# Casts of keys and queries and a first addition of values moved from VectorE to GpSimd, in two of four batches

## The chip, the cores and the metric

The kernel runs on one core of a Trainium2 chip. The time is the device time of one execution in microseconds, as the median of several runs. A core has TensorE (PE in the profile), VectorE (DVE), ScalarE (ACT), GpSimd (POOL) and SyncE (SP); SP issues most of the DMAs here. Each engine works through its own queue in order and waits on semaphores for the others.

## The reference, cut to what matters

Clustered attention, then a gated feed-forward network on its result. A query sees only the keys whose nearest centroid is the same as its own.

```python
# q, k, v: (4 batches, 8 heads, 768 tokens, 64), centroids: (8, 16, 64)
q_assign = np.argmax(np.einsum('bhsd,hcd->bhsc', q_n, c_n), axis=-1)
k_assign = np.argmax(np.einsum('bhsd,hcd->bhsc', k_n, c_n), axis=-1)
mask = q_assign[:, :, :, None] == k_assign[:, :, None, :]
scores = np.where(mask, scale * np.matmul(q, k.transpose(0, 1, 3, 2)), -1e9)
attn = np.exp(scores - np.max(scores, axis=-1, keepdims=True))
attn = attn / (np.sum(attn, axis=-1, keepdims=True) + 1e-09)
x = np.matmul(attn, v)            # then to (3072 tokens, 512)
gate = 1.0 / (1.0 + np.exp(-(x @ w_gate)))     # w_gate, w_val: (512, 1536)
out = (gate * (x @ w_val)) @ w_out             # w_out: (1536, 512)
```

## The kernel before

**Work and stages.** The four batches run one after the other, and in each four pairs of heads. A pair is 24 steps of attention, 12 a head in most cases; a step takes one block of 128 keys against 384 queries. PE computes scores (`sc`, L1066), ACT the exponentials (`es`, L1071), and PE the product with the values (`av`, L1089). After the last step of a head VectorE adds the precomputed sum of values to `av` (`t`, L372) and takes reciprocals (`rec`, L374), and GpSimd multiplies (the normalisation, `xp`, L377). SP transposes `xp` by DMA into `xTb` (L1120), from which the feed-forward network of the batch reads. Its matmuls (gate `g`, L532; value `v`, L548; output `o`, L865 and L994) fill the room between the attention steps of the next batch. The last batch ends with a closing part of its own from about 271 us on.

**Preparation of a pair.** Each of the pairs of the batches 2 to 4 (numbered b = 1 to 3 in the program), but for the first pair of b = 1, is prepared some 60 steps ahead by `pair_prep`. For each head e and side (keys, queries) `sp` splits the f32 input into a high half in f16 and the rest, side by side in one tile `hl`: a cast (L1631, 128 x 6 x 64 elements) and a subtraction (L1632, GpSimd) that reads the cast's result. `turn` transposes the whole `hl` by one DMA from SP into `T` (L412). PE multiplies `T` with the centroids (`lg`, L436 or L423), VectorE reduces and picks the nearest centroid (`lgs` L451, `mx` L462, `oh` L464 and L471), and SP transposes that by DMA (`ohT`, L1649) and copies its rows into `T` (L492), where they serve as additional rows of the score matmul. Scores of the pair then read `T`.

**Values.** `v_cast` casts a pair's values to f16 (`va`, L324, GpSimd). `v_sum` adds the six blocks of values of a pair in parts: `one` adds the first three blocks to the last three (L332), `two` adds the three results (L338, L339), and `rest` sums over partitions with a matmul (L343) and scales the result (L348). All of `one` and `two` run on VectorE.

**What sets the order.** The program is written out step by step. The table `SCHED` says by how many steps each piece of the preparation comes ahead of the pair's first use: an entry such as `b2p1sp10` for one pair, else `b2sp10` for b = 2 and 3, else a default. `sp` names a split, with head and side as its digits. Pieces due at a step are issued between that step's scores and the next. Each engine's queue holds its instructions in the order in which they are issued so. Inputs come in three buffers of each kind, `hl` has four. PSUM banks for scores, `lg`, `g` and `v` come from a ring of four, so that a matmul waits for whoever reads the bank used four allocations before.

Of the kernel before, what the change touches and what calls it, by code (L numbers as in the profile page):

```python
# [11 lines left out]
ALU = mybir.AluOpType  # L12
# [83 lines left out]
    "fwv": [354, 356, 357, 359, 364, 366, 370, 371], "b3p2pk1": -28.5, "END": 0,  # L96
}


# [1 line left out]
def kernel(  # L101
# [12 lines left out]
    PE, ACT, DVE, POOL, SP = nc.tensor, nc.scalar, nc.vector, nc.gpsimd, nc.sync  # L114
# [205 lines left out]
    def v_cast(b, p, cast=None, e=None):  # L320
        va = VA[b, p] = vas[(b * NP + p) % len(vas)]
        h = slice(0, 2) if e is None else slice(e, e + 1)
        done.update(("v", b, p, i) for i in range(2)[h])
        (cast or POOL.tensor_copy)(va[:, h, :, 0:64], RAW["v", b, p][:, h])  # L324

    def v_sum(b, p, eng=None):
        r, st = RAW["v", b, p], {}
        eng = eng or DVE

        def one():  # L330
            st["a"] = vsp.tile([128, 2, 3, 64], FP, tag="va3", name="va3")
            eng.tensor_tensor(st["a"], r[:, :, 0:3], r[:, :, 3:6], ALU.add)  # L332

        def two():
            a = st["a"]
            s = st["s"] = vss[(b * NP + p) % len(vss)]
            t = vsp.tile([128, 2, 64], FP, tag="va1", name="va1")
            eng.tensor_tensor(t, a[:, :, 0], a[:, :, 1], ALU.add)  # L338
            eng.tensor_tensor(s[:, :, 0:64], t, a[:, :, 2], ALU.add)  # L339

        def rest():
            t = (turns if SCHED.get(f"vso{b}{p}", SCHED.get(f"vso{p}", 0)) else bank)(130, FP, name="vs_ps")
            PE.matmul(  # L343
                out=t, lhsT=ones, rhs=st["s"].rearrange("p h d -> p (h d)"), start=True, stop=True
            )
            sv = svp.tile([128, 2, 65], FP, tag="sv", name="sv")
            SV[b, p] = sv
            DVE.tensor_scalar(sv.rearrange("p h d -> p (h d)"), t, TINY, None, ALU.mult)  # L348

        return one, two, rest  # L350
# [59 lines left out]
    def turn(key, hl, pl):  # L410
        T[key] = pl.tile([128, hl.shape[1], 128], HP, tag="T", name="T")
        SP.dma_start_transpose(out=T[key], in_=hl.rearrange("p c x -> p (c x)"))  # L412

    def logits2(groups, sep=False):

        lg = (turns if SCHED.get("lgop", 1) else bank)(512, FP, name="lg2")
        lx = sep and SCHED.get("lx", 0)
        seq = [(i, s) for i in range(len(groups)) for s in range(2)]
        if lx:
            seq = [(i, s) for s in range(2) for i in range(len(groups))]  # L420
        for i, s in seq:
            t, c, h = groups[i]
            PE.matmul(  # L423
                out=lg[:, bass.ts(i, NCL)], lhsT=t[:, c, :], rhs=cm[:, h, s, :],
                start=(i == 0 and s == 0), stop=(s == 1), skip_group_check=True,
            )
        return lg[:, 0 : len(groups) * NCL].rearrange("p (c n) -> p c n", n=NCL)

    def logits(t, h, n, copy=None):
        return logits1([(t, c, h) for c in range(n)], copy)  # L430
# [25 lines left out]
    def pick(lg, parts):  # L456

        if isinstance(lg, tuple):
            lg = join(*lg)
        n = lg.shape[1]  # L460
        mx = smp.tile([128, 18], FP, name="mx")
        DVE.tensor_reduce(mx[:, 0:n], lg, AX.X, ALU.max)  # L462
        for a, z, nh, key, o in parts:
            DVE.tensor_tensor(  # L464
                o,
                lg[:, a:z].rearrange("p (h c) n -> p h c n", h=nh),
                bcast(mx[:, a:z].rearrange("p (h c) -> p h c", h=nh), NCL),
                ALU.is_equal if key else ALU.is_lt,
            )
            if not key:  # L470
                DVE.tensor_scalar(o, o, MASK, None, ALU.mult)  # L471
# [4 lines left out]
    def new_oh():  # L476
        oh_n[0] += 1
        return ohs[oh_n[0] % 3]

    def oh_view(oh, slot, nh, step, nc_):  # L480

        v_ = oh.rearrange("p c (s x) -> p s c x", x=32)
        return v_[:, slot : slot + (nh - 1) * step + 1 : step, 0:nc_, 0:NCL]
# [7 lines left out]
    def hop(src, slot, t, c0, n):  # L491
        SP.dma_start(  # L492
            out=t[64:80, c0 : c0 + n, :], in_=src[32 * slot : 32 * slot + 16, 0:n, :]
        )
# [630 lines left out]
    def at(i, f):  # L1125
        bg.setdefault(max(i, step_no[0] - 0.5), []).append(f)
# [11 lines left out]
    def need(*names):  # L1138
        for n in names:
            assert n in done, n  # L1140
# [361 lines left out]
    a = P[0, 0, 0]  # L1502
# [121 lines left out]
    def pair_prep(b, p, use):  # L1624
        st = {}

        def sp(e, side):
            if side == 0:
                st["hl", e] = hlp.tile([128, 12, 128], HP, tag="hl", name="hl")
            hl, r = st["hl", e][:, 6 * side : 6 * side + 6], RAW["kq"[side], b, p][:, e]  # L1630
            DVE.tensor_copy(hl[:, :, 0:64], r)  # L1631
            POOL.tensor_tensor(hl[:, :, 64:128], r, hl[:, :, 0:64], ALU.subtract)  # L1632

        def lgt(e):
            t, h = T[b, 2 * p + e], 2 * p + e
            if SCHED.get(f"b{b}p{p}l2{e}", 0):
                st["lg", e] = logits2([(t, c, h) for c in range(12)])
            else:
                st["lg", e] = logits(t, h, 12, SCHED.get(f"b{b}p{p}le{e}", 0) and DVE.tensor_copy)

        def pk(e):
            if e == 0:
                st["oh"] = new_oh()
            pick(st["lg", e], [(0, 6, 1, True, oh_view(st["oh"], 2 * e, 1, 1, 6)),
                               (6, 12, 1, False, oh_view(st["oh"], 2 * e + 1, 1, 1, 6))])

        def ot():
            st["ot"] = ohp.tile([128, NCH, 128], HP, tag="ohT", name="ohT")
            SP.dma_start_transpose(out=st["ot"], in_=st["oh"].rearrange("p c x -> p (c x)"))  # L1649

        def hops(e):
            if SCHED.get("hop2", 0):
                SP.dma_start(
                    out=T[b, 2 * p + e][64:80].rearrange("x (s c) t -> s x c t", s=2),
                    in_=st["ot"].rearrange("(y x) c t -> y x c t", x=32)[2 * e : 2 * e + 2, 0:16],
                )
                return
            for s in range(2):
                hop(st["ot"], 2 * e + s, T[b, 2 * p + e], 6 * s, 6)

        def go(name, off, f):
            o = SCHED.get(f"b{b}p{p}{name}", SCHED.get(f"b2{name}", off) if b > 1 else off)

            def g():
                if name[:2] == "tn":
                    need((b, p, f"sp{name[2]}0"), (b, p, f"sp{name[2]}1"))
                if name == "ot":
                    need((b, p, "pk0"), (b, p, "pk1"))
                f()
                done.add((b, p, name))  # L1670

            at(use + o, g)

        for e in range(0 if (b, p) in PEP else 2):
            o = -58 + 10 * e
            go(f"sp{e}0", o, lambda e=e: sp(e, 0))
            go(f"sp{e}1", o + 4, lambda e=e: sp(e, 1))
            go(f"tn{e}", o + 9, lambda e=e: turn((b, 2 * p + e), st["hl", e], tp))
            go(f"lg{e}", o + 20, lambda e=e: lgt(e))
            go(f"pk{e}", o + 21, lambda e=e: pk(e))  # L1680
        if (b, p) not in PEP:
            go("ot", -26, ot)
            go("hp0", -16, lambda: hops(0))
            go("hp1", -15, lambda: hops(1))
        go("vc", -20, lambda: v_cast(b, p))
        go("vs", -10, lambda: (st.update(f=v_sum(b, p)), st["f"][0]()))
        go("vu", -8, lambda: st["f"][1]())
        go("vt", -6, lambda: st["f"][2]())
# [13 lines left out]
    for b in range(B):  # L1702
# [17 lines left out]
        for p, e, c in heads(b):  # L1720
            for s in head_steps(b, p, e, c):
# [4 lines left out]
                r = step_no[0] - BASE[b]  # L1726
# [44 lines left out]
```

## Time and profile before

| | |
|---|---|
| median of 3 runs | 319.14 us (319.08 to 319.54) |
| the profiled execution | 319.12 us, its span 317.3 us |
| PE | 310.0 us busy, 98% of the span |
| weight loads (PEld, beside PE) | 218.8 us, 69% |
| VectorE (DVE) | 238.6 us, 75% |
| ScalarE (ACT) | 244.9 us, 77% |
| GpSimd (POOL) | 120.9 us, 38% |
| granted TensorE clock | 1.00 throughout |

In a row of a timeline the first number is the start in us from the span's beginning, the second the duration; "x3" merges three equal instructions, and "[4.99 <-PE sc L1066]" gives the idle time of that engine before it and what ended that. In a row of groups stand the busy time in us and the mean length of one in ns, then the idle time before them. For DMAs a row of SP (SPq) is the time it takes to issue; when the data have landed is told apart.

### The profile page before, as it was taken

To read this page: it belongs to the slowest core of one execution; us is meant where nothing else is said; L and a number is where in the kernel's file an instruction comes from. 1 tells how busy PE (TensorE), PEld (TensorE's weight loads), DVE (VectorE), ACT (ScalarE), POOL (GpSimd) and SP (SyncE) were. 2 spreads that over 40 slices of the span, in tenths; PEclk is the share of its full clock that TensorE was granted. 3 is DMA by queue.
4 is the path that set the end of the run, shared out by engine and by line. 5 is a ranking of instruction groups with operands and counts; after the bars stand their busy time and mean duration, and the time that the engine had idled before them with its cause. 6 is when DMAs were issued, how large, how long until landed. Compare 5 with 4: busy or idle time off the path is not lost.

```text
span 317.3 us, 9228 instructions
## 1 busy us (share of the span) xinstructions
PE 310.0 (98%) x3492; PEld 218.8 (69%) x3492; DVE 238.6 (75%) x623; ACT 244.9 (77%) x555; POOL 120.9 (38%) x157
## 2 busy tenths in 40 slices
PE   7899999999999999999999999999999999999995
PEld 4688766766666666666777678766677678656685
DVE  5899756778688777686788688776888776678983
ACT  6688998797899887877776876777877887588621
POOL 5888454244434275423234333424212111026600
PEclk9999999999999999999999999999999999999999
DMA  7999998639848988976676455882506130300014
GB/s 196 379 259 169 271 164 143 176 83 264 242 100 163 204 221 136 199 217 161 106 193 153 151 118 134 248 153 53 112 2 76 55 27 14 145 1 3 0 35 165
DMA packets 77996, 45.16 MB, mean 142 GB/s; under 512 B 56896, under 2 KB 75520, under 8 KB 77952
## 3 DMA queue, kind: packets, MB, share of 16 engines
q1 hardware_dynamic: 73840, 39.66, 51.3%
q0 software_dynamic: 3680, 4.72, 9.1%
q8 instruction: 27, 0.44, 0.6%
q10 hardware_dynamic: 432, 0.20, 0.2%
q14 instruction: 17, 0.14, 0.1%
HBM read 28.34 MB, written 6.29 MB: 109 GB/s over the span
## 4 chain that ended last, share of the span: by engine, by line
PE 93%; DMA 2%; DVE 1%; POOL 1%; SPq 1%; issue 0%; ACT 0%; DVEq 0%
PE sc L1066 19%; PE g L532 15%; PE v L548 15%; PE av L1089 11%; PE o L994 9%; PE o L865 5%; PE lg L436 2%; PE o L699 2%; PE o_end L802 2%; PE av L699 2%; DMA kraw<-in_k_dram 2%; PE v L628 2%; PE y L699 2%; PE o L802 1%; PE av L802 1%; PE z L699 1%
## 5 line engine op out<-in xcount | busy, mean ns | idle before, releaser
L1071 ACT ACTIVATE es<-sc 128x384 f16<-128x384 f32 x384 | 174.1, 492 | 38.5 <-PE sc L1066 29.8
L1066 PE MATMUL sc<-T 128*128 128x384 f16 x384 | 117.3, 325 | 0.7 <-DVE T L1396 0.4
L1089 PEld LDWEIGHTS <-es 128*128 128x128 f16 x1152 | 81.3, 98 | 35.1 <-ACT es L1071 0.2
L1089 PE MATMUL av<-va,es 128*128 128x65 f16 x1152 | 97.6, 194 | 0.0
L553 DVE SCALAR_TENSOR_TENSOR hT<-th,v 128x384 f16<-128x384 f32 x72 | 39.8, 553 | 33.8 <-PE av L1089 29.6
L377 POOL TENSOR_TENSOR xp<-t,rec 128x384 f16<-128x384 f32 (+1 forms) x30 | 21.8, 726 | 97.3 <-DVE rec L374 49.2
L548 PE MATMUL v<-xTb,wv 128*128 128x384 f16 x288 | 58.5, 326 | 0.1
L532 PE MATMUL g<-xTb,wg 128*128 128x384 f16 x288 | 58.5, 326 | 0.0
L538 ACT ACTIVATE th<-g 128x384 f32<-128x384 f32 x72 | 35.4, 492 | 8.3 <-PE g L532 6.3
L1066 PEld LDWEIGHTS <-T 128*128 128x128 f16 x384 | 37.0, 96 | 1.2 <-DVE T L1396 0.7
L548 PEld LDWEIGHTS <-wv 128*128 128x128 f16 x288 | 28.0, 97 | 13.9 <-issue 0.3
L532 PEld LDWEIGHTS <-wg 128*128 128x128 f16 x288 | 27.9, 97 | 13.9
L1632 POOL TENSOR_TENSOR hl<-kraw,hl 128x384 f16<-128x384 f32 x22 | 20.2, 920 | 40.6 <-DVE hl L1631 25.9
L1632 POOL TENSOR_TENSOR hl<-qraw,hl 128x384 f16<-128x384 f32 x22 | 21.1, 961 | 11.1 <-DVE hl L1631 11.1
L865 PE MATMUL o<-wo,hT 128*128 128x512 f16 x72 | 19.9, 379 | 0.0
L372 DVE TENSOR_TENSOR t<-av,sv 128x390 f32<-128x390 f32 (+1 forms) x30 | 14.4, 480 | 7.1 <-PE av L1089 5.3
L941 DVE TENSOR_TENSOR ob<-o,ob 128x256 f32<-128x256 f32 (+1 forms) x28 | 15.0, 549 | 4.7 <-PE o L994 3.2
L708 POOL TENSOR_TENSOR hT<-T 128x384 f16<-128x384 f32 x12 | 11.8, 1001 | 16.2 <-DVE T L657 15.6
L994 PE MATMUL o<-wo,hT 128*128 128x256 f16 x108 | 16.8, 272 | 0.0
L994 PEld LDWEIGHTS <-sum 128*128 128x128 f16 x144 | 14.0, 97 | 3.3
L451 DVE TENSOR_REDUCE lgs<-lg 128x192 f32<-128x384 f32 x23 | 12.7, 551 | 3.0 <-PE lg L436 2.9
L324 POOL CAST va<-vraw 128x768 f16<-128x768 f32 x15 | 13.1, 873 | 2.4 <-DMA vraw<-in_v_dram 2.4
(225 smaller groups left out, 470.2 us busy)
## 6 DMA issues: line engine op xcount, KB each, us to landing
vraw<-in_v_dram SPq DMA_DIRECT2D x15, 384.0 KB, 4.9
kraw<-in_k_dram SPq DMA_DIRECT2D x14, 384.0 KB, 4.2
qraw<-in_q_dram SPq DMA_DIRECT2D x12, 384.0 KB, 4.1
out_dram<-ob SPq DMA_DIRECT2D x17, 256.0 KB, 2.2
wg<-in_moe_w_gate_dram POOLq DMA_DIRECT2D x2, 768.0 KB, 9.2
wv<-in_moe_w_val_dram POOLq DMA_DIRECT2D x2, 768.0 KB, 10.4
wo<-in_moe_w_out_dram POOLq DMA_DIRECT2D x2, 768.0 KB, 9.3
T<-ohT SPq DMA_DIRECT2D x44, 24.0 KB, 1.9
```

What stands on the lines that cost most here:

```text
L377: (eng or POOL).tensor_tensor(x, t[:, 0:nq, 0:64], bcast(rec[:, 0:nq], 64), ALU.mult)
L532: PE.matmul(out=g[:, 0:n], lhsT=wg[fc // WQ][:, dc, fc % WQ, :], rhs=xT[:, dc, t0 : t0 + n], start=(dc == 0), stop=(dc == NDC - 1),)
L538: ACT.activation(th[:, 0:n], g[:, 0:n], AF.Tanh)
L548: PE.matmul(out=w[:, 0:n], lhsT=wv[fc // WQ][:, dc, fc % WQ, :], rhs=xT[:, dc, t0 : t0 + n], start=(dc == 0), stop=(dc == NDC - 1),)
L553: DVE.scalar_tensor_tensor(HB[b, blk][:, fc, 0:n], st[0][:, 0:n], 1.0, w[:, 0:n], ALU.add, ALU.mult)
L699: PE.matmul(out=o, lhsT=l, rhs=r, start=start and d == 0, stop=stop and d == 1, skip_group_check=True,)
L865: PE.matmul(out=o, lhsT=HB[b, blk][:, fc, bass.ts(t, 128)], rhs=wo[fc // WON][:, fc % WON, :], start=(fc == 0), stop=(fc == NFC - 1),)
L994: PE.matmul(out=st[z][:, e], lhsT=a[:, c, :], rhs=rhs[:, c, :], start=start and c + e == 0, stop=c == HF - 1, skip_group_check=True,)
L1066: PE.matmul(out=sc.rearrange("p (c t) -> p c t", t=128), lhsT=s["k"], rhs=s["q"], start=True, stop=True,)
L1071: ACT.activation(es, sc, AF.Exp, scale=SCALE)
L1089: PE.matmul(out=av[:, a0 + s["c0"] + i, :], lhsT=s["es"][:, bass.ts(i, 128)], rhs=VA[b, p][:, e, s["j"], :], start=(first and i == 0 and a ...
L1632: POOL.tensor_tensor(hl[:, :, 64:128], r, hl[:, :, 0:64], ALU.subtract)
```

## The change

In the batches b = 2 and 3 the cast of `sp` and the first addition of `v_sum` go to GpSimd; b = 1 stays. The entries for these splits come 1.5 steps sooner (before: -57.5, -54, -50.0, -44.5 by the entries for b = 2). Since the eight pairs of two heads and two sides have 32 casts, and each pair has one first addition, 40 instructions change their engine.

```diff
-    "fwv": [354, 356, 357, 359, 364, 366, 370, 371], "b3p2pk1": -28.5, "END": 0,
+    "fwv": [354, 356, 357, 359, 364, 366, 370, 371], "b3p2pk1": -28.5, "pc": (2, 3), "pv": (2, 3),
+    "b2p0sp00": -59.0, "b2p0sp01": -55.5, "b2p0sp10": -51.5, "b2p0sp11": -46.0,
...
+    "b3p3sp00": -59.0, "b3p3sp01": -55.5, "b3p3sp10": -51.5, "b3p3sp11": -46.0, "END": 0,
...
-            eng.tensor_tensor(st["a"], r[:, :, 0:3], r[:, :, 3:6], ALU.add)
+            (POOL if b in SCHED["pv"] else eng).tensor_tensor(st["a"], r[:, :, 0:3], r[:, :, 3:6], ALU.add)
...
-            DVE.tensor_copy(hl[:, :, 0:64], r)
+            (POOL if b in SCHED["pc"] else DVE).tensor_copy(hl[:, :, 0:64], r)
             POOL.tensor_tensor(hl[:, :, 64:128], r, hl[:, :, 0:64], ALU.subtract)
```

On GpSimd, in the preparation of the third batch's second pair (b = 2, pair 1, heads 0 and 1 in the tiles hl_2834 and hl_2927 before, hl_2811 and hl_2915 now):

```order
 L377 TENSOR_TENSOR xp_2655<-t_2806,rec_2808 128x6x64
-L1632 TENSOR_TENSOR hl_2834<-kraw_2595,hl_2834 128x6x64
+L1631 COPY hl_2811<-kraw_2598 128x6x64
+L1632 TENSOR_TENSOR hl_2811<-kraw_2598,hl_2811 128x6x64
 L324 COPY va2_169<-vraw_2008 128x12x64
-L1632 TENSOR_TENSOR hl_2834<-qraw_2597,hl_2834 128x6x64
-L1632 TENSOR_TENSOR hl_2927<-kraw_2595,hl_2927 128x6x64
+L1631 COPY hl_2811<-qraw_2600 128x6x64
+L1632 TENSOR_TENSOR hl_2811<-qraw_2600,hl_2811 128x6x64
+L1631 COPY hl_2915<-kraw_2598 128x6x64
+L1632 TENSOR_TENSOR hl_2915<-kraw_2598,hl_2915 128x6x64
 L377 TENSOR_TENSOR xp_2655<-t_2957,rec_2959 128x6x64
```

Each subtraction now has its cast in front of it on the same engine, and both stand behind the same normalisation (L377) and the same cast of values (L324) as the subtraction alone did.

A few rows further on GpSimd, the first of the moved additions (into va3_3009):

```order
-L1632 TENSOR_TENSOR hl_2927<-qraw_2597,hl_2927 128x6x64
+L1631 COPY hl_2915<-qraw_2600 128x6x64
+L1632 TENSOR_TENSOR hl_2915<-qraw_2600,hl_2915 128x6x64
+L332 TENSOR_TENSOR va3_3009<-vraw_2174 128x384
 L377 TENSOR_TENSOR xp_2967<-t_3029,rec_3031 128x3x64
```

The addition stands between the last subtraction of that pair and the next normalisation. On VectorE the same stretch of the program, from the cast of the queries of the second head on, before:

```order
L1631 COPY hl<-qraw 128x6x64
L348 TENSOR_SCALAR sv<-vs_ps 128x130
L332 TENSOR_TENSOR va_3009<-vraw 128x384
L372 TENSOR_TENSOR t<-av,sv 128x195
L374 RECIPROCAL rec<-t 128x3
L338 TENSOR_TENSOR va_3035<-va_3009 128x128
L339 TENSOR_TENSOR vs_163<-va_3035,va_3009 128x2x64
L451 TENSOR_REDUCE lgs<-lg 128x192
```

And on VectorE now:

```order
L348 TENSOR_SCALAR sv<-vs_ps 128x130
L372 TENSOR_TENSOR t<-av,sv 128x195
L374 RECIPROCAL rec<-t 128x3
L338 TENSOR_TENSOR va_3035<-va_3009 128x128
L339 TENSOR_TENSOR vs_163<-va_3035,va_3009 128x2x64
L451 TENSOR_REDUCE lgs<-lg 128x192
```

The cast and the addition are gone, and L338 now waits for GpSimd. The order on PE, ACT and SP is the same as before.

1 row of the table SCHED is left out of this document.

## The prediction

> **What bounds the kernel now.** I read the page first: busy shares and the chain that ended last.
>
> ```profile
> PE 310.0 (98%) x3492; PEld 218.8 (69%) x3492; DVE 238.6 (75%) x623; ACT 244.9 (77%) x555; POOL 120.9 (38%) x157
> ...
> PE 93%; DMA 2%; DVE 1%; POOL 1%; SPq 1%; issue 0%; ACT 0%; DVEq 0%
> ```
>
> The matrix engine is busy 98% of the span and carries 93% of the chain. The engine that the change relieves, VectorE (DVE), is busy 75% and stands for 1%. The moved work lies between about 97 and 230 us, so next comes the table of windows for that stretch (PE, weight loads, DVE, ACT, POOL).
>
> ```profile
> 97.00:230.00 133.00, 132.93 (x1485) 91.94 (x1482) 99.56 (x264) 106.27 (x241) 50.39 (x60) 1.00 0.71 161
> ```
>
> PE is busy 132.93 of 133 us at a granted clock of 1.00. The ends of matmuls are modelled, so this could still hide gaps; the timeline shows whether it does.
>
> ```profile
> 123.61 0.32 PE L1066 MATMUL sc<-T 128*128 128x384 f16 x1
> 123.77 0.26 PE L1089 MATMUL av<-va,es 128*128 128x65 f16 x3
> ...
> 126.17 0.46 PE L436 MATMUL lg<-cm,T 128*128 128x32 f16 x12
> ...
> 183.53 0.33 PE L1066 MATMUL sc<-T 128*128 128x384 f16 x1
> ...
> 183.92 0.81 PE L548 MATMUL v<-xTb,wv 128*128 128x384 f16 x4
> ```
>
> A score matmul is drawn 0.32 us long, but the next matmul starts 0.16 us after it: PE streams, and a wait would show as a longer distance. Reading the distances through the stretch, I find one clear gap: at 183.53 the next start comes after 0.39 us, so 0.23 us are lost. So PE sets the end, nothing in this stretch holds it up, and there is about 0.2 us to be won. The change can gain next to nothing; the question is whether it makes PE wait.
>
> **The change part by part.** PE's, ACT's and SP's order stays; VectorE loses 32 casts (L1631) and 8 additions (L332), and POOL (GpSimd) gets them. The prices (busy us and mean ns; the row with three numbers has shortest, median and longest):
>
> ```profile
> L1631 DVE CAST hl<-qraw 128x384 f16<-128x384 f32 x22 | 9.0, 410 | 0.0
> L1631 DVE CAST hl<-kraw 128x384 f16<-128x384 f32 x22 | 8.4, 382 | 0.0
> L332 DVE TENSOR_TENSOR va<-vraw 128x384 f32<-128x384 f32 x12 | 7.3, 611 | 0.0
> ...
> L1631 DVE CAST hl<-kraw x22: 323/350/955, 44.0 to 218.3; 128x384 f16<-128x384 f32 x22
> ...
> L1411 POOL CAST hl<-qraw 128x384 f16<-128x384 f32 x2 | 1.0, 509 | 0.0
> L1632 POOL TENSOR_TENSOR hl<-qraw,hl 128x384 f16<-128x384 f32 x22 | 21.1, 961 | 11.1 <-DVE hl L1631 11.1
> L377 POOL TENSOR_TENSOR xp<-t,rec 128x384 f16<-128x384 f32 x18 | 15.6, 868 | 73.8 <-DVE rec L374 33.3 <-DMA T<-ohT 18.1 <-issue 14.9
> ```
>
> Removed from VectorE: 32 x 0.396 + 8 x 0.611 = 17.6 us. PE does not wait for VectorE here, so this is worth 0 on the path; at most it closes the 0.23 us gap, whose cause the profile does not name. I count 0 and keep 0.23 as the bound of the gain.
>
> Added to POOL: a cast of this very shape takes 0.51 us there. No POOL row shows an addition of f32 into f32; two-input instructions of the same size take 0.87 (L377) to 0.96 (L1632), and I take 0.9. How a cast and its subtraction (L1632) follow each other on POOL is shown early in the program:
>
> ```profile
> 13.53 0.50 POOL L1287 CAST hl<-kraw 128x384 f16<-128x384 f32 x1
> 14.12 0.91 POOL L1294 TENSOR_TENSOR hl<-kraw,hl 128x384 f16<-128x384 f32 x1
> 14.97 0.34 POOL L1287 CAST hl<-qraw 128x192 f16<-128x192 f32 x1
> ```
>
> The subtraction starts 0.59 us after its cast starts, and the next instruction 0.85 us after that. So each cast puts 0.59 us in front of its subtraction: 32 x 0.59 + 8 x 0.9 = 26 us more on POOL, whose 50.39 us of 133 become about 76. It has the time on average; what counts is its queue, place by place. The 1.5 steps do not help there: the order shows that no cast passes a normalisation (L377) that its subtraction stood behind before, so a normalisation still lets the whole run of casts and subtractions go, now longer.
>
> A later subtraction delays the DMA transpose of `hl` into `T` (L412), which SP issues in order, and PE's assignment matmuls (L436, `lg`) read `T`. I went through the pairs of heads for the distance from that landing to those matmuls. It is thinnest in the third batch, pair 1:
>
> ```profile
> 111.57 0.82 POOL L377 TENSOR_TENSOR xp<-t,rec 128x384 f16<-128x384 f32 x1 [4.99 <-PE sc L1066]
> 112.36 0.91 POOL L1632 TENSOR_TENSOR hl<-kraw,hl 128x384 f16<-128x384 f32 x1
> 113.21 0.95 POOL L324 CAST va<-vraw 128x768 f16<-128x768 f32 x1
> 114.13 0.91 POOL L1632 TENSOR_TENSOR hl<-qraw,hl 128x384 f16<-128x384 f32 x1
> ...
> 117.64 0.84 POOL L377 TENSOR_TENSOR xp<-t,rec 128x384 f16<-128x384 f32 x1 [0.79 <-DVE rec L374]
> ```
>
> ```profile
> 115.07 2.08 SPq L412 DMA_TRANSPOSE T<-hl  x1
> 117.24 1.25 SPq L1649 DMA_TRANSPOSE ohT<-oh  x1
> 118.58 2.17 SPq L1120 DMA_TRANSPOSE xTb<-xp  x1
> 120.84 0.53 SPq L504 DMA_DIRECT2D out_dram<-ob  x1
> 121.48 1.47 SPq L412 DMA_TRANSPOSE T<-hl  x1
> ...
> 125.61 1.26 SPq L1120 DMA_TRANSPOSE xTb<-xp  x1
> ```
>
> Before, POOL subtracts at 112.36 and 114.13 right behind the normalisation, and SP issues the transpose at 115.07, the moment the second ends. Now two casts stand between: 112.36 cast, 112.95 subtract, 113.80 cast of values, 114.72 cast, 115.31 to 116.22 subtract. The transpose moves from 115.07 to 116.26: 1.19 us. SP's rows are back to back (115.07 + 2.08 = 117.15, next 117.24, and so on), so what is queued behind it moves as well: the transposes of `ohT` and `xTb`, a store, and the second head's transpose at 121.48. That one lands:
>
> ```profile
> L412 SPq DMA_TRANSPOSE T<-hl x1: 1473/1473/1473, 121.5 to 121.5; - x1
> ...
> DMA to landing us min/median/max: 4.2/4.2/4.2
> ```
>
> 121.48 + 4.2 = 125.68, and PE's `lg` starts at 126.17: 0.49 us of cover. If all SP rows keep their lengths, the landing comes at 126.87 and PE waits 0.70 us, which it never gets back. If the rows of 2.08 and 2.17 us shorten to the 1.47 and 1.26 that the same transposes show elsewhere in this list, 1.5 us are won back and PE waits 0. The long rows follow the raw loads; the load of values waits for the cast of 113.21, so moves by 0.59 against the transpose's 1.19, and 0.6 us more lie between them. I take half of that, 0.3, as won: a wait of 0.4 us, nearer to the rows as they stand.
>
> The Trainium skill (GPSIMD Engine Reference, 4.1 Engine selection) calls one-input work on GpSimd roughly line-rate and two-input work about twice as slow as VectorE. Here a cast takes 0.51 there against a median of 0.35 on VectorE, so the trace decides for the dearer price; at an estimated 0.32 us from that page's clock and 384 elements the wait would be 0.4 us smaller, that is, none.
>
> The moved additions: the first stands between the second head's last subtraction (cast at 118.45, subtraction 119.0 to 119.9) and the next normalisation, so ends at 120.8. VectorE's next addition (L338) waits for it, and behind that the `lgs` sum (L451) that frees the bank of `lg`:
>
> ```profile
> 120.55 0.26 DVE L338 TENSOR_TENSOR va<-va 128x128 f32<-128x128 f32 x1
> ...
> 121.29 0.54 DVE L451 TENSOR_REDUCE lgs<-lg 128x192 f32<-128x384 f32 x1
> ...
> 122.67 0.33 PE L1066 MATMUL sc<-T 128*128 128x384 f16 x1
> ```
>
> L338 moves by 0.25 us; L451 ended at 121.83 and the bank is wanted by the fourth one behind it, at 122.67: 0.84 us of cover. Cost 0, and if that cover went, the excess over 0.84. The `xTb` transpose of 125.61, late by the same shift, feeds a gate matmul:
>
> ```profile
> 128.52 0.81 PE L532 MATMUL g<-xTb,wg 128*128 128x384 f16 x4
> ...
> DMA to landing us min/median/max: 2.4/2.4/2.4
> ```
>
> It lands at 128.01, read by the fourth of these four (128.52 + 3 x 0.16 = 129.00): 1.0 us of cover, plus whatever PE has already waited. Cost 0. In the next pair the transposes have the longest flights:
>
> ```profile
> 128.06 2.02 SPq L412 DMA_TRANSPOSE T<-hl  x1
> ...
> DMA to landing us min/median/max: 3.2/4.0/6.3
> ...
> 136.15 0.30 PE L436 MATMUL lg<-cm,T 128*128 128x32 f16 x6
> ```
>
> Even with the maximum of 6.3 us it lands at 134.4, 1.75 before its reader; a shift of 1.2 leaves 0.55. The later pairs stand further off in the same reading. Cost 0.
>
> Sum against the profiled execution (319.12, its span 317.3; the median is 319.14): 0.4 of wait at 126 us, nothing else: **319.5**. Its own range runs from 0.23 of gain to the 0.64 of loss named next: 318.9 to 319.76. A measurement of this kernel can tell about 0.2%, that is 0.64 us, from no change.
>
> **The rivals.**
>
> *The late transposes, in full.* If SP's rows keep their lengths, the wait is already 0.70; the case is slower once the transpose of 121.48 moves by more than 0.49 + 0.64 = 1.13 us. If casts and subtractions lengthen each other by a third on the way (0.4 us more), the wait is 1.1: 320.2. For it: SP has no slack from 115 to 126. Against: 1.5 us of its rows there are longer than their like. 33%.
>
> *VectorE held by POOL.* A cast on VectorE that meets POOL's subtraction takes more than twice the median of 0.35:
>
> ```profile
> 112.66 0.82 DVE L1631 CAST hl<-qraw 128x384 f16<-128x384 f32 x1
> ```
>
> With 26 us more on POOL, the additions that stay on VectorE (L338, L339) meet it more often. If two of them near 120.6 each wait for a POOL instruction of 0.9 us, L451 is late by 1.8, 0.96 beyond its cover: 320.1. Against: the casts that suffered are gone, and 17.6 us with them. 4%. By the Trainium skill (SBUF — State Buffer, "SBUF: two separate sides") GpSimd and a VectorE instruction with two SBUF inputs exclude each other for the whole instruction; the row of 112.66 agrees.
>
> *Faster.* VectorE's relief closes the gap at 183.5 and nothing is late: 318.9, still within 0.2%. To pass 0.2% more must be won than I find. 6%.
>
> **How the numbers follow.** The forecast (a wait between 0 and 0.64) has 57%, the late transposes 33%, VectorE held 4%, faster 6%. Slower: 33 + 4 = 37%. The range goes from the closed gap (318.9) to just above the full delay (320.4).
>
> **What would show it.** Right: POOL's second subtraction behind the normalisation of 111.6 ends near 116.2, SP's transpose is issued at once, the one after it near 122.4, and PE's `lg` of 126.17 starts 0.2 to 0.6 us later than streaming would have it; PE distances elsewhere unchanged. Wrong: that transpose still at 121.5 and no wait (same, nearer 319.0); PE gaps at other places, above all before scores whose bank VectorE frees; or a PE total that shrinks by more than 0.3 us.

## The result, and the profile after

The changed kernel takes 321.14 us in the median of its five runs (320.82 to 322.14) beside 319.08 of before in the same series: a ratio of 1.0067 with an interval of 1.0048 to 1.0087. A second series gave 320.88 beside 319.08, 1.0056 (1.0035 to 1.0076). So it is slower by 1.8 to 2.1 us, where the forecast was 0.4 and the range ended at 320.4.

Two profiled executions of the changed kernel are read here. The first took 322.14 us; its start was disturbed by 0.46 us (the granted clock was 0.5 for 3.4 us at about 14 us), so all its times stand that much later. The second took 320.58 us, with a start like that of before. The page of the first, busy shares and chain:

```profile
PE 311.6 (97%) x3492; PEld 219.8 (69%) x3492; DVE 230.8 (72%) x583; ACT 244.9 (76%) x555; POOL 144.0 (45%) x197
...
PE 87%; DVE 4%; DMA 4%; POOL 2%; issue 1%; SPq 1%; ACT 0%; DVEq 0%; POOLq 0%
```

PE fell from 93% of the chain to 87%, and VectorE, which was relieved, rose from 1% to 4%. The table of windows of the second, for the stretch that the prediction read (PE, weight loads, DVE, ACT, POOL):

```profile
97.00:230.00 133.00, 132.31 (x1468) 91.08 (x1467) 90.44 (x220) 104.90 (x237) 72.62 (x99) 1.00 0.71 161
```

GpSimd is busy 72.62 us instead of 50.39, near the 76 forecast, and VectorE 90.44 instead of 99.56. PE, which had run 1485 matmuls in these 133 us, runs 1468 at the same granted clock of 1.00. The view of waits of the first, from 95 to 235 us, names where PE stands (total us, times, longest):

```profile
PE lg L436 <- DMA T<-hl: 1.2, 1, 1.2
...
DVE va L338 <- POOL va L332: 0.9, 2, 0.6
...
PE sc L1066 <- DVE hT L553: 0.2, 1, 0.2
PE g L532 <- DVE hT L553: 0.2, 1, 0.2
```

These numbers are small beside what was lost, since ends of matmuls are modelled late. From here on, lost time of PE is worked out from starts: the distance between two matmul starts beyond the distance of the same two in the first profile of before. By that measure PE loses time in two ways.

**One late landing.** SP's transpose of `hl` for the first head of the third batch's pair 1, and PE's `lg` that reads it; first the first profile of the changed kernel, from its timeline:

```profile
116.94 2.26 SPq L412 DMA_TRANSPOSE T<-hl  x1
...
121.49 0.26 PE L1089 MATMUL av<-va,es 128*128 128x65 f16 x3
122.92 0.47 PE L436 MATMUL lg<-cm,T 128*128 128x32 f16 x12 [1.17 <-DMA T<-hl]
```

Then the second:

```profile
116.38 1.71 SPq L412 DMA_TRANSPOSE T<-hl  x1
...
120.94 0.26 PE L1089 MATMUL av<-va,es 128*128 128x65 f16 x3
121.35 0.47 PE L436 MATMUL lg<-cm,T 128*128 128x32 f16 x12 [0.15 <-DMA T<-hl]
```

The `lg` starts 1.43 us behind the product before it in the first and 0.41 in the second, where before had 0.10 (120.65 to 120.75): 1.33 and 0.32 lost.

**Five short waits for VectorE**, near 103, 156, 175, 186 and 220 us: 0.34, 0.15, 0.34, 0.23 and 0.08 us in the first profile, 0.38, 0.15, 0.34, 0.23 and 0.08 in the second, 1.2 us together in both. The one at 175 in the second profile's timeline, VectorE, GpSimd and PE:

```profile
171.76 1.37 DVE L911 TENSOR_TENSOR sum<-sum,hT 128x768 f16<-128x768 f16 x1
173.05 1.17 DVE L913 TENSOR_TENSOR sum<-hT 128x768 f16<-128x768 f16 x1
...
175.00 0.55 DVE L553 SCALAR_TENSOR_TENSOR hT<-th,v 128x384 f16<-128x384 f32 x1
...
171.69 1.02 POOL L332 TENSOR_TENSOR va<-vraw 128x384 f32<-128x384 f32 x1
172.65 1.17 POOL L324 CAST va<-vraw 128x768 f16<-128x768 f32 x1
...
175.09 0.32 PE L1066 MATMUL sc<-T 128*128 128x384 f16 x1
175.60 0.48 PE L532 MATMUL g<-xTb,wg 128*128 128x384 f16 x2 [0.18 <-DVE hT L553]
```

The same place before, from its timeline:

```profile
170.99 0.92 DVE L911 TENSOR_TENSOR sum<-sum,hT 128x768 f16<-128x768 f16 x1
171.84 0.55 DVE L913 TENSOR_TENSOR sum<-hT 128x768 f16<-128x768 f16 x1
...
173.63 0.55 DVE L553 SCALAR_TENSOR_TENSOR hT<-th,v 128x384 f16<-128x384 f32 x1
...
170.68 0.82 POOL L324 CAST va<-vraw 128x768 f16<-128x768 f32 x1
...
174.33 0.32 PE L1066 MATMUL sc<-T 128*128 128x384 f16 x1
174.49 0.81 PE L532 MATMUL g<-xTb,wg 128*128 128x384 f16 x4
```

Before, GpSimd's cast of values (L324) ends at 171.50, L911 is held in part (0.92), L913 runs free (0.55), and the `hT` that frees a bank for PE starts at 173.63. Now a cast and an addition stand in front of L324. Both additions of the feed-forward sums on VectorE are held, L911 while L332 runs and L913 until the end of L324 at 173.82, and although VectorE has lost its own L332 here, `hT` starts at 175.00. PE's gate matmul follows its score at 0.51 us instead of 0.16.

### The profile page after: what moved, and what is told of

Its sections match the earlier page's. It is cut to its first block, busy times and chain, and to the rows that moved or that the text cites. A ratio compares the mean times of both kernels' runs of the same rounds, so it can differ in the third digit from the quotient of the medians.

```text
span 320.3 us, 9190 instructions
## 1 busy us (share of the span) xinstructions
PE 311.6 (97%) x3492; PEld 219.8 (69%) x3492; DVE 230.8 (72%) x583; ACT 244.9 (76%) x555; POOL 144.0 (45%) x197
## 4 chain that ended last, share of the span: by engine, by line
PE 87%; DVE 4%; DMA 4%; POOL 2%; issue 1%; SPq 1%; ACT 0%; DVEq 0%; POOLq 0%
PE sc L1066 18%; PE g L532 14%; PE v L548 14%; PE av L1089 10%; PE o L994 8%; PE o L865 4%; PE o L699 2%; PE lg L436 2%; DMA T<-hl 2%; PE o_end L802 2%; PE av L699 2%; DMA kraw<-in_k_dram 2%; PE y L699 2%; PE v L628 2%; PE o L802 1%; PE av L802 1%
## 5 line engine op out<-in xcount | busy, mean ns | idle before, releaser
L553 DVE SCALAR_TENSOR_TENSOR hT<-th,v 128x384 f16<-128x384 f32 x72 | 39.8, 552 | 39.6 <-PE av L1089 34.8
L377 POOL TENSOR_TENSOR xp<-t,rec 128x384 f16<-128x384 f32 (+1 forms) x30 | 21.6, 720 | 103.8 <-DVE rec L374 89.7
L451 DVE TENSOR_REDUCE lgs<-lg 128x192 f32<-128x384 f32 x23 | 12.7, 550 | 4.5 <-PE lg L436 4.5
L324 POOL CAST va<-vraw 128x768 f16<-128x768 f32 x15 | 13.6, 909 | 2.3 <-DMA vraw<-in_v_dram 2.3
```

The lines of the kernel that those rows point to most:

```text
L377: (eng or POOL).tensor_tensor(x, t[:, 0:nq, 0:64], bcast(rec[:, 0:nq], 64), ALU.mult)
L553: DVE.scalar_tensor_tensor(HB[b, blk][:, fc, 0:n], st[0][:, 0:n], 1.0, w[:, 0:n], ALU.add, ALU.mult)
```

## The experiments

Times are medians; "lost" is PE's lost time in the profiled execution, worked out as above.

| kernel | us | beside before | ratio (95%) | lost near 121 | lost at the five places |
|---|---|---|---|---|---|
| changed, first series | 321.14 | 319.08 | 1.0067 (1.0048 to 1.0087) | 1.33 | 1.15 |
| changed, second series | 320.88 | 319.08 | 1.0056 (1.0035 to 1.0076) | 0.32 | 1.19 |
| before again | 319.06 | 319.08 | one run | 0.37 | 0 |
| casts only | 320.44 | 319.29 | 1.0033 (1.0020 to 1.0045) | 0.62 | 0.57 |
| additions only | 319.62 | 319.29 | 1.0011 (0.9994 to 1.0028) | 0.12 | 0.14 |
| all but the casts of b2p1 | 320.40 | 319.29 | 1.0040 (1.0025 to 1.0056) | 0.63 | 1.05 |
| casts of b2p1 alone | 319.51 | 319.29 | 1.0007 (0.9990 to 1.0024) | 0.58 | 0 |
| copies on GpSimd | 321.34 | 319.08 | 1.0063 (1.0045 to 1.0081) | 0 | see below |
| fills on GpSimd | 320.13 | 319.08 | 1.0034 (1.0019 to 1.0050) | 1.03 | see below |
| changed, b2p1 earlier | 320.32 | 319.13 | 1.0034 (1.0022 to 1.0047) | 0 | 1.22 |
| changed, 14 back | 319.92 | 319.13 | 1.0022 (1.0010 to 1.0034) | 0.66 | 0 |
| both of these | 319.54 | 319.13 | 1.0011 (0.9996 to 1.0026) | 0 | 0 |
| before, b2p1 earlier | 319.12 | 319.13 | 1.0002 (0.9992 to 1.0013) | 0 | 0 |

### The casts alone, the additions alone

```diff
-"pc": (2, 3), "pv": (2, 3)
+"pc": (2, 3), "pv": ()          # casts only
+"pc": (), "pv": (2, 3)          # additions only, splits at their old steps
```

> The changed kernel without the moved additions: the 32 casts on GpSimd, the 8 first additions back on VectorE. Late-transpose theory (the casts ahead of the subtractions of the third batch's pair 1 make the DMA transpose late, PE waits at the first lg of that pair): the wait of 1.3 us at about 121 us stays, so 320.4 to 320.9. Port theory (GpSimd's longer occupation holds VectorE's two-input and f16 instructions, and PE waits for a bank): casts are 19 of the 26 us added on GpSimd, so most of the waits at 103, 158, 177, 187 us stay as well: 320.5 to 321.0. Addition theory (L338 waiting for GpSimd's addition is what holds PE): back to 319.1 to 319.4.

> The kernel before with only the 8 first additions on GpSimd, casts and their steps as before. Late-transpose theory: no cast stands ahead of a subtraction, so within 0.2 us of before, 318.9 to 319.3. Port theory: 7 of the 26 us are added on GpSimd, and each addition now meets VectorE's sums: some 0.3 us, 319.2 to 319.6. Addition theory: the whole loss, 321.

The casts cost 1.15 us, the additions 0.33, which their interval does not tell from nothing. Their profiles show that the two are not independent: at 175 us PE loses 0 with the casts alone, 0.11 with the additions alone and 0.34 with both, and at 186 neither alone loses anything, both 0.23. What each puts in front of the next GpSimd instruction adds up, and only the sum pushes it onto the VectorE instruction that PE waits for. The profile of the additions alone also loses 0.24 us at the `lg` near 100 and 0.28 at the one near 127, both behind a transpose of `hl` whose splits are as before.

### The pair that the prediction named, left out and alone

```diff
-(POOL if b in SCHED["pc"] else DVE)
+(POOL if b in SCHED["pc"] and (b, p) != (2, 1) else DVE)    # all but b2p1
+(POOL if (b, p) == (2, 1) else DVE)                         # b2p1 alone, additions on VectorE
```

The entries of the splits whose casts are back on VectorE are at their old steps.

> The changed kernel with the 4 casts of one pair (third batch, pair 1) back on VectorE at their old steps; 28 casts and 8 additions stay on GpSimd. Late-transpose theory: the wait at the lg of 121 us goes, 1.3 us of the profiled 2.5: 319.7 to 320.0. Port theory: the smaller waits at 103, 158, 177 and 187 us stay (1.1 us in the profile): the same 319.7 to 320.2. If the late transpose were not that pair's own doing (raw loads in its way by chance), 320.8 to 321.1.

> The kernel before with only the 4 casts of the third batch's pair 1 on GpSimd, 1.5 steps sooner. Late-transpose theory: the subtraction ends 1.2 us later, PE waits 0.7 to 1.3 us at the pair's first or second lg: 319.8 to 320.4. Port theory: 4 casts of 32 are nothing: 319.1 to 319.2.

Without this pair's casts most of the loss stays (1.0040), and alone they cost 0.2 us, within the interval of nothing. In the first, the transpose is issued at 115.40, nearly as early as before (115.07), and its `lg` still waits 0.63 us: the flight was 6.3 us in that execution, against 4.2 in the first profile of before. So the wait near 121 us is not only a matter of late casts.

### A second profile of both kernels

> The changed kernel as it is, for a second profile and a narrower ratio. If its loss is fixed by the program (casts late at the first head of the third batch's pair 1, and VectorE's sums lengthened beside GpSimd), the ratio is again 1.005 to 1.008 and the trace shows the same two kinds of idle time of TensorE: 0.5 to 1.4 us at the first lg of that pair near 121 us, and 0.1 to 0.35 us each near 103, 158, 176, 187 and 221 us, 1.0 to 1.2 us together. If the late landing near 121 us was chance of one execution, its gap there is under 0.2 us and the ratio under 1.004.

> Before as it is, one more profile, for the flight of the first transposed tile of the third batch's pair 1 (4.25 us in the first profile, its lg not waiting). If the flight changes from run to run by itself, it lies between 3.5 and 6.5 us, and above 5.7 us TensorE waits at that lg near 121 us here too. If later issue is what makes it longer, it is again 4.0 to 4.5 us and there is no wait there.

The five short waits of the changed kernel are the same to 0.04 us in both executions; the wait near 121 us is 1.33 and 0.32. And before itself waits there, from its second profile's timeline:

```profile
114.62 2.10 SPq L412 DMA_TRANSPOSE T<-hl  x1
...
120.68 0.47 PE L436 MATMUL lg<-cm,T 128*128 128x32 f16 x12 [0.21 <-DMA T<-hl]
```

It was issued 0.45 us sooner than in the first profile, as this execution runs about 0.5 us ahead from its start on, and landed 1.3 us later. The view of that instruction gives its flight, in the first profile of before and then in the second:

```profile
DMA to landing us min/median/max: 4.2/4.2/4.2
```

```profile
DMA to landing us min/median/max: 6.0/6.0/6.0
```

The next two kernels equal before up to about 141 us and add two more executions: flights of 4.8 and 6.7 us, waits of 0 and 1.03. Over these four the mean wait is (0 + 0.37 + 0 + 1.03) / 4 = 0.35 us; over the five with this pair's casts on GpSimd and its steps unchanged (both profiles of the changed kernel, casts only, b2p1 alone, 14 back) it is (1.33 + 0.32 + 0.62 + 0.58 + 0.66) / 5 = 0.70. By this estimate from nine executions the later issue costs about 0.35 us on average. Two more kernels keep this pair's casts on VectorE: the additions alone wait 0.12 and all but b2p1 0.63, and with them the mean of before becomes 0.36. But single waits reach from 0 to 1.03 on the one side and from 0.32 to 1.33 on the other, so a difference of 0.35 is not shown by so few; b2p1 alone, the direct test, measured 0.2 us with an interval that holds nothing.

### More of GpSimd's work without moving any

In before, ahead of each of the last 20 subtractions (pairs from b2p3 on), two copies, or two fills:

```diff
+            if b * NP + p >= 11:
+                for _ in range(2):
+                    POOL.tensor_copy(hl[:, :, 64:128], r)      # copies
+                    POOL.memset(hl[:, :, 64:128], 0.0)         # or fills
             POOL.tensor_tensor(hl[:, :, 64:128], r, hl[:, :, 0:64], ALU.subtract)
```

> Before, with two further copies of the same raw keys or queries on GpSimd ahead of each of the last 20 subtractions (pairs from the third batch's pair 3 on), written where the subtraction writes afterwards; VectorE keeps its casts. Their subtractions have 3.5 us and more of cover. Contention theory (VectorE's additions and sums that lie beside GpSimd's reads of SBUF are held): VectorE's f16 sums L909 to L913, L339 and L464 in that stretch grow from 0.55 to 0.8-1.2 us where they overlap, TensorE idles 0.1 to 0.35 us at several places after 150 us, and the time is 0.4 to 1.5 us above before. Queue theory (only GpSimd's own work that comes later counts): about 1 us more in front of each subtraction is covered, 0 to 0.3 us above before, and the same as with the fills.

> Before, with two fills of the same places by a constant on GpSimd ahead of each of the same 20 subtractions: instructions of the same number and extent of output that read nothing. Contention theory, if reads count: VectorE's sums stay near 0.55 us and the time is 0 to 0.3 us above before. If writes alone hold VectorE too, it loses as the copies do, 0.4 to 1.5 us. Queue theory: the same as the copies, within 0.2 us.

The copies lose 2.26 us, more than expected, with VectorE relieved of nothing: PE loses 0.59 near 156, 0.54 near 175, 0.27 near 204, 0.65 near 220 and 0.10 at 147. The fills lose 1.05. That lies in the range that was given for the case that writes hold VectorE too (0.4 to 1.5), but they lose less than half of what the copies do, and not by holding VectorE where PE waits: PE loses 0.37 near 156 and 0.31 near 175, told below, and 1.03 at the `lg` near 121, which lies ahead of all the fills. At 220 us, a copy in the timeline of the kernel with copies, beside VectorE:

```profile
219.22 0.55 DVE L464 TENSOR_TENSOR oh<-lgs,mx 128x96 f16<-128x96 f32 x1
219.81 0.46 DVE L471 TENSOR_SCALAR oh<-oh 128x96 f16<-128x96 f16 x1
...
219.13 1.10 POOL L1634 CAST hl<-kraw 128x384 f16<-128x384 f32 x2
```

Here the copies themselves hold VectorE. Near 156 and 175 fills and copies do the same: they push the later subtraction and cast of values onto L911 and L913, which in the kernel with fills take 1.06 and 1.17 us. So both theories were too simple. By these profiles it is neither the load nor the queue by itself: work in front of a GpSimd instruction moves it in time, and it costs where it lands on a VectorE instruction that it can hold and that PE is about to need.

### Curing the two losses apart and together

The first edit moves the first head's casts and subtractions of b2p1 to where GpSimd idles, and its transpose ahead of three raw loads on SP. The second gives 14 of the 40 instructions back to VectorE, those ahead of the five places.

```diff
-"b2p1sp00": -59.0, "b2p1sp01": -55.5,
+"b2p1sp00": -68, "b2p1sp01": -66, "b2p1tn0": -60,
```

```diff
+"cb": {(2, 0, 0, 0), (2, 0, 0, 1), (2, 0, 1, 0), (2, 3, 1, 1), (3, 0, 1, 1), (3, 1, 0, 0),
+       (3, 1, 0, 1), (3, 1, 1, 0), (3, 3, 0, 0), (3, 3, 0, 1), (3, 3, 1, 0)},   # casts back: b, p, head, side
+"vb": {(2, 2), (2, 3), (3, 0)},                                                 # additions back
```

> The changed kernel, with the first head's casts and subtractions of the third batch's pair 1 some 9 steps sooner still, ahead of a normalisation, where GpSimd idles for 5 us, and its transposed load ahead of three loads of raw inputs on SyncE's queue. Theory (two separate losses: the late landing at that head's lg, 0.3 to 1.3 us, and VectorE held beside GpSimd at five places, 1.2 us): the idle time of TensorE near 121 us is gone, the five others stay, and the time is 0.3 to 0.9 us below the changed kernel, 0.9 to 1.5 above before. Rival (the late landing is the whole loss): the time of before, within 0.3 us.

> The changed kernel, with 14 of its 40 instructions back on VectorE: those that push a GpSimd instruction onto the VectorE instruction that the traces show held near 103, 156, 175, 186 and 220 us (casts of pairs b2p0, b3p1 and b3p3 for three of four halves, one cast each of b2p3 and b3p0, additions of b2p2, b2p3 and b3p0). Theory (place decides): the idle time at these five places falls from 1.2 to 0.2 us or less, and the time is 0.9 to 1.2 us below the changed kernel, with the wait near 121 us as before. Rival (the load on GpSimd decides, each moved instruction at the same price): 14/40 of 1.8, so 0.6 us below. Rival (VectorE's holds are covered): no difference.

> Both edits together. Theory (two separate losses that add): no idle time near 121 us and 0.2 us or less at the five places; the time of before within 0.4 us, 318.8 to 319.5 us beside 319.1. If a third loss exists, over 0.5 us above before.

With the first edit SP issues the transpose at 110.87, and PE's `lg` follows its predecessor at 0.10 us again, from that kernel's timeline:

```profile
110.87 1.44 SPq L412 DMA_TRANSPOSE T<-hl  x1
...
120.45 0.26 PE L1089 MATMUL av<-va,es 128*128 128x65 f16 x3
120.55 0.46 PE L436 MATMUL lg<-cm,T 128*128 128x32 f16 x12
```

The time stays 1.19 us above before; in its profile the five places lose 1.22, and 0.17 is lost anew at 122.6 (told below, under the miss). With the second edit these five are gone; the place at 175, from its timeline, is that of before again:

```profile
171.81 0.93 DVE L911 TENSOR_TENSOR sum<-sum,hT 128x768 f16<-128x768 f16 x1
172.65 0.55 DVE L913 TENSOR_TENSOR sum<-hT 128x768 f16<-128x768 f16 x1
...
171.50 0.82 POOL L324 CAST va<-vraw 128x768 f16<-128x768 f32 x1
...
175.14 0.32 PE L1066 MATMUL sc<-T 128*128 128x384 f16 x1
175.30 0.81 PE L532 MATMUL g<-xTb,wg 128*128 128x384 f16 x4
```

It is 1.0 us faster than the changed kernel of the second series and 1.2 than that of the first (theory 0.9 to 1.2; by load, 0.6), though 26 of the 40 instructions are still on GpSimd. The intervals of the two ratios are too wide to tell 1.0 from 0.6; what speaks against the load is the profile, in which all five places are back at the distances of before. It has a new loss of 0.44 us near 98 us: a cast given back to VectorE meets a normalisation on GpSimd there (L1631 takes 0.98 us at 96.86) and makes `hT` late. With both edits the time is 0.41 us above before, no longer told from it; its profile keeps that new loss (0.43) and the 0.17 at 122.8, and nothing else of size. The kernel with the first edit alone, which differs from this one by the 14 instructions, takes 320.32 against 319.54. The difference of 0.78 is what the profiles give for it: the five places (1.22) less the new loss near 98 (0.43). The gain by the first edit (319.92 to 319.54 beside the second) is no larger than the scatter of the runs.

### Before, with the transpose earlier

```diff
+"b2p1sp00": -62, "b2p1sp01": -60, "b2p1tn0": -60,
```

> Before (casts and additions on VectorE), with the first head's casts and subtractions of the third batch's pair 1 some 4 to 6 steps sooner, and its transposed load ahead of the three raw loads. Before waited at that head's lg 0 us in one profile and 0.37 us in another: if the landing varies, the edit gains 0.1 to 0.4 us, with no idle time near 121 us. If the first profile is the rule, no difference (within 0.2 us). If the later loads of raw inputs matter, it is slower by 0.2 us or more.

The `lg` no longer waits in the profile, its time of 318.67 to 319.99 has the same median. The gain of 0.35 us that four executions of before suggest did not show; the interval reaches from 0.26 us of gain to 0.41 of loss. Whether the sooner transpose costs elsewhere what it saves is open. No version here beats before. The 1.5 steps were not tried by themselves.

## Why the prediction was wrong, point by point

**PE bound, nothing to win: right.** VectorE's busy time in the span fell from 238.6 to 230.8 us, and PE gained nothing. But it fell by 7.8 where 17.6 had been taken off: what stayed on VectorE became longer. By the lines of the two profiles (before, and the second of the changed kernel) L471 takes 2.0 us more in all, L338 1.5, L464 1.3, L911 and L339 0.9 each. The gap at 183.5, the bound of the gain, stayed at 0.23 in every profile.

**The prices on GpSimd: right, but for the addition.** From the view of lines of the changed kernel's first profile:

```profile
L1631 POOL CAST hl<-kraw 128x384 f16<-128x384 f32 x16 | 8.7, 544 | 0.0
L332 POOL TENSOR_TENSOR va<-vraw 128x384 f32<-128x384 f32 x8 | 8.1, 1014 | 0.0
```

The addition takes 1.01 us instead of the 0.9 taken; a cast 0.50 where it meets nothing.

**The chain in the pair b2p1: right to 0.15 us.** In the second profile, from its timeline:

```profile
111.85 0.82 POOL L377 TENSOR_TENSOR xp<-t,rec 128x384 f16<-128x384 f32 x1 [5.25 <-PE sc L1066]
112.62 0.50 POOL L1631 CAST hl<-kraw 128x384 f16<-128x384 f32 x1
...
115.44 0.91 POOL L1632 TENSOR_TENSOR hl<-qraw,hl 128x384 f16<-128x384 f32 x1
```

The second subtraction ends at 116.35 (forecast 116.22) and the transpose is issued at 116.38 (forecast 116.26).

**Which transpose binds: wrong.** The prediction set its wait of 0.4 us at the second head's `lg`, near 126. That one never waited in the changed kernel: its transpose was issued at 122.88 and 122.22 and took 3.4 and 3.3 us, not the 4.2 that one execution had shown, and the wait of the first head had pushed its reader back. (With the additions alone it did wait, by 0.28 us, behind a flight of 5.1.) The first head's transpose does not stand in the prediction; at its flight of 4.2 us it would have kept about 0.3 of cover at the new issue. Behind the raw loads that flight is not a constant: it was between 4.2 and 6.7 us. The step that failed here is a single flight used as a price with a cover of tenths. That the estimate of 0.35 us lies near the forecast 0.4 is luck: it is another transpose, and single executions lost up to 1.33.

**PE distances elsewhere unchanged: wrong, and this is the miss.** The sum put the cost of VectorE at nothing; the mechanism stood among the rivals only, as VectorE held by GpSimd, with 4%, put at the additions near 120.6. There L338 waited 0.27 us and PE lost nothing in the changed kernel. But PE was already late there by its wait at the `lg`. In the kernel with the first edit, where that wait is gone, the named place does cost, from its timeline:

```profile
120.72 0.58 DVE L338 TENSOR_TENSOR va<-va 128x128 f32<-128x128 f32 x1 [0.28 <-POOL va L332]
...
121.33 0.80 DVE L339 TENSOR_TENSOR vs<-va,va 128x128 f16<-128x128 f32 x1
...
122.05 0.55 DVE L451 TENSOR_REDUCE lgs<-lg 128x192 f32<-128x384 f32 x1
...
122.38 0.25 PE L1089 MATMUL av<-va,es 128*128 128x65 f16 x3
...
122.64 0.32 PE L1066 MATMUL sc<-T 128*128 128x384 f16 x1
```

L338 waits and takes 0.58 instead of 0.26, L339 0.80 instead of 0.52. L451 ends 2.05 us behind the start of the `lg`, 1.08 before: 0.97 later, beyond the cover of 0.84. The score for whose bank L451 was priced starts 0.04 behind that end and loses 0.17, and the same in the kernel with both edits.

The price was worked out at that one place, the one where VectorE waits for GpSimd's result. A hold needs no dependence: it came at `oh` (L471, L464) and the feed-forward sums (L909, L911, L913), which read nothing that moved, and at the last addition of values (L339), which reads the moved addition's result but had it: that addition ended at 183.92, and the L338 ahead of L339 started at 184.16. That makes five places whose cover did not suffice, and 1.2 of the 1.8 to 2.1 us. So the step that failed is the cost of VectorE, put at nothing everywhere but in one rival at one place, and the runs showed 1.2 us at five others in its stead. The argument against it, that the casts which suffered were gone, counted the holds that were removed and not those that were moved.

The Trainium skill (SBUF — State Buffer, "SBUF: two separate sides") says that the one of the two engines that starts first keeps the shared ports for its whole instruction, and that this concerns VectorE instructions with two SBUF inputs against a GpSimd instruction that reads SBUF, and those in a two-port mode. The runs agree on the first group: L913 with both inputs in SBUF takes 1.17 us instead of 0.55. They agree on what is spared too: L553, one of whose inputs is in PSUM, has a mean of 552 ns over 72 in the changed kernel and 553 before. The row of 112.66 that the prediction set beside the rule is a cast with one input, so it is no case of that group. Had the prediction laid the rule along VectorE's whole queue, and not beside one pair of additions, these places could have come into sight.

**What is left.** 0.35, an estimate, and 1.2 make 1.55 of the measured 1.8 to 2.1 us. The rest lies within the intervals of both series.

## What to carry to other kernels

Where two engines can hold each other, the busy time that an instruction takes from one and brings to the other says little: lay the moved instructions, and all that they push back in their queue, beside the other engine's queue in time, and look at each instruction there whose result the bounding engine needs next. A cover of tenths of a microsecond read from one execution is no cover where a DMA flight stands in it; look at a second profile before pricing it. A part taken alone can look free, as the additions did, and cost through the delay that it adds to the others.

## What the runs showed of the hardware that was not expected

The hold is nearly whole. From the timeline of the changed kernel's second profile, near 185 us, and of the kernel with 14 back, at the same place:

```profile
184.55 0.96 DVE L339 TENSOR_TENSOR vs<-va,va 128x128 f16<-128x128 f32 x1
...
184.45 0.91 POOL L1632 TENSOR_TENSOR hl<-kraw,hl 128x384 f16<-128x384 f32 x1
```

```profile
184.15 0.30 DVE L339 TENSOR_TENSOR vs<-va,va 128x128 f16<-128x128 f32 x1
```

An addition of 0.30 us ends at 185.51, 0.15 us after the subtraction that started 0.10 before it. An f16 scalar operation with one input (L471) is held like the additions; its shortest, median and longest in the first profile of the changed kernel:

```profile
L471 DVE TENSOR_SCALAR oh<-oh x22: 186/189/894, 64.7 to 239.9; 128x96 f16<-128x96 f16 x22
```

GpSimd is held as well: its cast of 128x768 values takes 0.82 us where it meets nothing, and 1.17 in the row of 172.65, where it begins while L911 still runs, until 173.13. The flight of one transpose of 128x12x128 f16 behind three raw loads on SP's queue was 4.2 and 6.0 us in two executions of before and 4.8 and 6.7 in two kernels that equal it up to there; issued ahead of the loads, it was 3.2 to 3.7 us in three kernels.
